# Turning q in 32x32 blocks on VectorE instead of by TensorE and DMA, in an attention + maxout kernel

## The chip, the cores and the metric

One core of a Trainium2 chip. The metric is the device time of one execution in microseconds (us), the median of several. Where I give a start or a duration from a profile, it is one profiled execution of that kernel. Engines: PE is TensorE, PEld its weight loads, DVE VectorE, ACT ScalarE, POOL GpSimd, SP SyncE.

## The reference

Eight batches of low-rank attention, followed by a maxout feed-forward layer over the same tokens. Cut to what matters:

```python
# q, k, v: [8 batches, 8 heads, 1024 tokens, 64] float32;  E, F: [64, 1024]
k_proj = einsum('ks,bhsd->bhkd', E, k)          # 1024 keys become 64
v_proj = einsum('ks,bhsd->bhkd', F, v)
scores = q @ k_proj^T / 8                       # contraction over d = 64
attn   = softmax(scores) @ v_proj
x      = attn with heads side by side           # [8192, 512]
h      = max(x @ w1, x @ w2, x @ w3)            # w: [512, 768]
out    = h @ w_out                              # w_out: [768, 512]
```

The contraction of the scores runs over d. The kernel's score matmuls read q and the keys with d on the partitions (in the trace of the kernel before, a moving operand of 64x512: 64 d by 512 tokens). So q, which is loaded with tokens on the partitions, is turned until d lies there. How q is turned is what changes here.

## The kernel before

It is a software pipeline: while the feed-forward matmuls of batch b run, the attention of batch b+1 is slipped between them in numbered *slots*. In the stage studied here one slot follows each group of four layer-1 matmuls (one PSUM bank, 4 x 216 ns = 0.86 us). Layer 1 rotates through four PSUM banks (0 to 3), which ACT and DVE empty; attention uses banks 4 to 7. Batch 0 has its own start-up code, which the change leaves alone.

Before the change q is turned in two ways. Batch 1, whose q is the last of its three inputs to be loaded, by 32 PE transposes through PSUM; batches 2 to 7 by DMA transposes, two per batch, issued by SP:

```python
def q_turn(b, hs):                                    # batches 2 to 7
    nc.sync.dma_start_transpose(
        out=qT[b % NB][:, hs].rearrange("p h s t -> p (h s) t"),
        in_=q_t[b % NB][:, hs].rearrange("p h si d -> p (h si d)"))

def q_pe1(hh):                                        # batch 1, two calls
    for h in range(4 * hh, 4 * hh + 4):
        for sp in range(SI // 2):
            o = (h % 2) * 512 + sp * P
            nc.tensor.transpose(out=psb[:, AB + (h % 4) // 2, o:o + P],
                                in_=q_t[1][:, h, 2 * sp:2 * sp + 2, :].rearrange("p s d -> p (s d)"), identity=ident)
    for j in range(2):                                # PSUM to SBUF, one on ACT, one on DVE
        (nc.vector.tensor_copy if j else nc.scalar.copy)(
            out=qT[1][:, ...], in_=psb[:, AB + j, :])
```

Keys and scores. The 64 projected keys leave PSUM twice, so that a copy lies on either half of the partitions after a DMA transpose; a score group is 8 matmuls in a 64x64 tiling (two waves of four tiles; in the trace the four of a wave start 3 to 4 ns apart, and the second wave 240 ns after the first):

```python
def kv():
    # ... 16 matmuls: keys to partitions 0-63, values to 64-127 of bank AB = 4
    nc.scalar.copy(out=kp2[i][:, :, 0, :], in_=kv_k)          # ACT, from PSUM
    nc.vector.tensor_copy(out=kp2[i][:, :, 1, :], in_=kv_k)   # DVE, from PSUM
    turn(i)                                                   # SP: DMA transpose kpT <- kp2
    nc.scalar.copy(out=vp2[i][KP:P], in_=kv_v[:, 1])
    nc.vector.tensor_copy(out=vp2[i][0:KP], in_=kv_v[:, 0])

def scores(u):
    for gg in range(2):
        g = 2 * u + gg
        for par in range(2):
            r = slice(par * D, (par + 1) * D)
            for col in range(2):
                h = HEAD[2 * g + col]
                nc.tensor.matmul(out=ps[col * KP:(col + 1) * KP, AB + 2 * gg + par, :],
                                 lhsT=kpT[i][r, h, :], rhs=qT[i][r, h, :, :], start=True, stop=True)
    # ... Exp on ACT, two instructions
```

Layer 1 and its evictions, and the schedule of batch 1's attention:

```python
# l1: four matmuls into one of four banks, then
if i == 0:   nc.scalar.copy(out=h1s[jt % 2], in_=ps[:, bank, :])                                        # ACT
elif i == 1: nc.vector.tensor_tensor(out=m12[jt % 2], in0=ps[:, bank, :], in1=h1s[jt % 2], op=ALU.max)  # DVE
else:        nc.vector.tensor_tensor(out=hT[c % 2][:, jt, :], in0=ps[:, bank, :], in1=m12[jt % 2], op=ALU.max)

# b == 0: (slot, work); g1[0] is kv of batch 1, g1[1] and g1[2] its two score groups
groups = [..., (20, g1[0]), (22, lambda: q_pe1(0)), (24, lambda: q_pe1(1)), (25, g1[1]), (28, g1[2]), ...]
```

The softmax here doesn't subtract the row's maximum and nothing guards it: scores larger than these inputs give would overflow.

Of the kernel before, what the change touches and what calls it, by code (L numbers as in the profile page):

```python
# [16 lines left out]
def kernel(ctx: ExitStack, tc: tile.TileContext, q, k, v, E, F, w1, w2, w3, w_out, out):  # L17
    nc = tc.nc
# [30 lines left out]
    q_t = [T([P, H, SI, D], BF16, f"q_t{i}") for i in range(NB)]  # L49
    qT = [T([P, H, SI // 2, P], BF16, f"qT{i}") for i in range(NB)]  # L50
    kp2 = [T([KP, H, 2, D], BF16, f"kp2_{i}") for i in range(NB)]
    kpT = [T([P, H, KP], BF16, f"kpT{i}") for i in range(NB)]
    vp2 = [T([P, NPAIR, 2, D // 2], BF16, f"vp2_{i}") for i in range(NB)]
    pT = T([P, NPAIR, 2, 512], BF16, "pT")
    xT = [T([P, NCT, 2, 512], BF16, f"xT{i}") for i in range(3)]
    lns = [T([P, 1024], FP32, f"lns{i}") for i in range(2)]
# [18 lines left out]

    out_v = out.rearrange("(b p sp par) m -> b par p sp m", p=P, sp=SI // 2, par=2)
    out_0 = out.rearrange("(b ch m t) n -> b ch m t n", ch=2, m=P, t=4)[0]
# [11 lines left out]
    def load_behind_turn(b, order="qkv"):  # L89

        nc.gpsimd.tensor_copy(out=seen, in_=kpT[(b - 1) % NB][:, 0, 0:1])
        for c in order:
            load(b, *{"q": (q, q_t), "k": (k, k_t), "v": (v, v_t)}[c])

    def q_turn(b, hs):
        nc.sync.dma_start_transpose(
            out=qT[b % NB][:, hs].rearrange("p h s t -> p (h s) t"),
            in_=q_t[b % NB][:, hs].rearrange("p h si d -> p (h si d)"),
        )
# [11 lines left out]
    def attention(b, turn):  # L111
        i = b % NB

        def kv():
            for si in range(SI):
                nc.tensor.matmul(out=ps[0:KP, AB, :], lhsT=eT[:, si, :], rhs=k_t[i][:, :, si, :],  # L116
                                 start=(si == 0), stop=(si == SI - 1))
                nc.tensor.matmul(out=ps[KP:P, AB, :], lhsT=fT[:, si, :], rhs=v_t[i][:, :, si, :],  # L118
                                 start=(si == 0), stop=(si == SI - 1))
            kv_k = ps[0:KP, AB, :].rearrange("p (h d) -> p h d", d=D)  # L120
            kv_v = ps[KP:P, AB, :].rearrange("p (g u dd f) -> p u g f dd", u=2, f=2, dd=HD)
            nc.scalar.copy(out=kp2[i][:, :, 0, :], in_=kv_k)  # L122
            nc.vector.tensor_copy(out=kp2[i][:, :, 1, :], in_=kv_k)  # L123
            turn(i)
            nc.scalar.copy(out=vp2[i][KP:P], in_=kv_v[:, 1])
            nc.vector.tensor_copy(out=vp2[i][0:KP], in_=kv_v[:, 0])

        def scores(u):
            for gg in range(2):
                g = 2 * u + gg  # L130
                for par in range(2):
                    r = slice(par * D, (par + 1) * D)
                    for col in range(2):
                        h = HEAD[2 * g + col]
                        nc.tensor.matmul(out=ps[col * KP:(col + 1) * KP, AB + 2 * gg + par, :],  # L135
                                         lhsT=kpT[i][r, h, :], rhs=qT[i][r, h, :, :], start=True, stop=True)
            for gg in range(2):
                nc.scalar.activation(out=pT[:, 2 * u + gg, :, :], in_=ps[:, AB + 2 * gg:AB + 2 * gg + 2, :],  # L138
                                     func=AF.Exp, scale=scale)

# [16 lines left out]
        def av(half):  # L157
            quads(lambda rows, g: vp2[i][rows, g, half, :])
            for u in range(2):
                nc.vector.tensor_tensor(out=xT[b % 3][:, 2 * u + half, :, :], in0=ps[:, AB + 2 * u:AB + 2 * u + 2, :],  # L160
                                        in1=rinv[u].rearrange("p (c n) -> p c n", c=2), op=ALU.mult)
# [4 lines left out]
    def turn_dma(i):  # L166
        nc.sync.dma_start_transpose(out=kpT[i], in_=kp2[i].rearrange("p h c d -> p (h c d)"))

# [7 lines left out]
    def l1(b, ch, c, jt, i):  # L176
        bank = fbank()
        for ct in range(NCT):
            nc.tensor.matmul(out=ps[:, bank, :], lhsT=w_sb[i][:, ct, jt * P:(jt + 1) * P],  # L179
                             rhs=xT[b % 3][:, ct, ch, :], start=(ct == 0), stop=(ct == NCT - 1))  # L180
        if i == 0:
# [50 lines left out]
    def k_proj0(g):  # L232
        for si in range(SI):
            for u in range(2):
                nc.tensor.matmul(out=ps[u * D:(u + 1) * D, 2, g * KP:(g + 1) * KP], lhsT=k_t[0][:, HEAD[2 * g + u], si, :],
                                 rhs=eT[:, si, :], start=(si == 0), stop=(si == SI - 1))
        nc.vector.tensor_copy(out=kpT[0][:, g, :], in_=ps[:, 2, g * KP:(g + 1) * KP])

# [7 lines left out]
    def scores0(ch, g, bank):  # L246
        for u in range(2):
            rows = slice(u * D, (u + 1) * D)
            nc.tensor.matmul(out=ps[u * KP:(u + 1) * KP, bank, :], lhsT=kpT[0][rows, g, :],  # L249
                             rhs=qT[0][rows, 4 * ch + g, :, :], start=True, stop=True)  # L250

# [20 lines left out]
    def q_up0():  # L272
# [5 lines left out]
        for j in range(2):  # L278
            (nc.vector.tensor_copy if j else nc.scalar.copy)(
                out=qT[0][:, 4 + 2 * j:6 + 2 * j].rearrange("p h s t -> p (h s t)"),  # L280
                in_=ps[:, 4 + 2 * j:6 + 2 * j, :].rearrange("p b n -> p (b n)"))
# [7 lines left out]
    def av_up0():  # L289
# [3 lines left out]
        norm0(1, 1, 4, (0, 1))  # L293


    def q_pe1(hh):
        for h in range(4 * hh, 4 * hh + 4):
            for sp in range(SI // 2):
                o = (h % 2) * 512 + sp * P
                nc.tensor.transpose(out=psb[:, AB + (h % 4) // 2, o:o + P],  # L300
                                    in_=q_t[1][:, h, 2 * sp:2 * sp + 2, :].rearrange("p s d -> p (s d)"), identity=ident)
        for j in range(2):
            (nc.vector.tensor_copy if j else nc.scalar.copy)(
                out=qT[1][:, 4 * hh + 2 * j:4 * hh + 2 * j + 2].rearrange("p h s t -> p (h s t)"), in_=psb[:, AB + j, :])

# [49 lines left out]
    def q_turn0(g):  # L355
        for n in range(4):
            nc.tensor.transpose(out=psb[:, 4 + g, n * P:(n + 1) * P],
                                in_=q_0[:, n, 2 * g:2 * g + 2, :].rearrange("p h d -> p (h d)"), identity=ident)
        nc.vector.tensor_copy(out=qT[0][:, g].rearrange("p s t -> p (s t)"), in_=psb[:, 4 + g, 0:512])

# [87 lines left out]
    for b in range(B):  # L448
        groups = attention(b + 1, turn_dma) if b + 1 < B else []
        if b == 0:  # L450
            g1 = [g for _, g in groups]
            groups = [(9, scores_up0), (12, lambda: sums0(1, 4)), (20, g1[0]), (22, lambda: q_pe1(0)), (24, lambda: q_pe1(1)), (25, g1[1]), (28, g1[2]),
                      (31, g1[3]), (32, g1[4]), (33, g1[5]), (34, g1[6]), (36, g1[7])]
# [3 lines left out]
        def tick():  # L457
# [5 lines left out]
            if b == 0:  # L463
                if slot == 22:
                    load_behind_turn(2, "kvq")
                if slot == 28:
                    q_turn(2, slice(0, H // 2))
                return
            if b == 1 and slot == 3:
                q_turn(2, slice(H // 2, H))  # L470
            if b + 2 < B:
                if slot == 9:
                    load_behind_turn(b + 2)
                if slot == 18:
                    q_turn(b + 2, slice(0, H // 2))
                if slot == 27:
                    q_turn(b + 2, slice(H // 2, H))

# [58 lines left out]
```

## Time and profile before

| | before |
|---|---|
| median time | 400.27 us (400.25 to 400.53, 3 runs) |
| span of the profiled run | 398.1 us |
| PE busy | 392.5 us, 99% of the span |
| steady period of one batch | 46.70 us |
| from batch 1's keys to batch 2's keys | 27.05 us |
| from batch 2's keys to batch 3's keys | 41.52 us |
| batch 1's keys to the last matmul | 346.81 us |

The last four rows are distances between starts of the same matmuls, which don't depend on how long the loads at the start took.

From the profile page of the kernel before, the busy time of each engine and three of the rows of tenths by slice of the span (9 is 90% or more):

```profile
PE 392.5 (99%) x2432; PEld 170.0 (43%) x2432; DVE 186.9 (47%) x269; ACT 166.0 (42%) x249; POOL 71.6 (18%) x110
...
PE   8999999999999999999999999999999999999996
...
DVE  3347355453834365443843266342654338433441
...
PEclk9999999999999999999999999999999999999999
```

PE has no idle slice at full clock, and DVE is half idle. The same page's row of DMA queue 1 (packets, MB, share of 16 engines), its chain of work by engine, and the DVE row of the second key copy (busy us, mean ns, then idle time before and its releaser):

```profile
q1 hardware_dynamic: 30032, 8.92, 15.3%
...
PE 95%; DMA 2%; DVE 1%; ACT 0%; POOL 0%; issue 0%; POOLq 0%; DVEq 0%
...
L123 DVE CAST kp<-ps 64x512 bf16<-64x512 f32 x7 | 4.8, 683 | 12.6 <-ACT kp L122 12.6
```

The chain that ended last is 95% PE, so a saving off PE is worth nothing unless it removes a PE wait. In the view of groups of instructions by form, the PE transposes and the score matmuls of the kernel before:

```profile
L135 PE MATMUL ps<-qT,kpT 64*64 64x512 bf16 x112 | 8.8, 388 | 0.0
...
L300 PE MATMUL ps<-ident,q_t 128*128 128x128 bf16 x32 | 2.1, 219 | 0.4 <-DVE vp L126 0.4
```

PE never waits before the scores (idle 0.0), and waits 0.4 us before the transposes. The timeline of PE in the stage of batch 1's attention (start, us, engine, line, operation, count, and idle time just before):

```profile
49.64 1.90 PE L179 MATMUL ps<-xT,w_sb 128*128 128x512 bf16 x8
51.95 1.05 PE L300 MATMUL ps<-ident,q_t 128*128 128x128 bf16 x16 [0.42 <-DVE vp L126]
52.84 1.89 PE L179 MATMUL ps<-xT,w_sb 128*128 128x512 bf16 x8
54.57 1.06 PE L300 MATMUL ps<-ident,q_t 128*128 128x128 bf16 x16
55.47 1.03 PE L179 MATMUL ps<-xT,w_sb 128*128 128x512 bf16 x4
56.42 0.63 PE L135 MATMUL ps<-qT,kpT 64*64 64x512 bf16 x8
```

The two transpose groups cost 0.89 us each (51.95 to 52.84), and the first one waits for the bank that the keys and values leave (the releaser is the value copy, L126). These 2.2 us are all that the change can take from PE.

### The profile page before, as it was taken

The page shows a single profiled execution, that of the slowest core. Times are in us where ns is not written, and L with a number is a line of the kernel's source. Part 1 is how long each engine was busy: PE and PEld are TensorE (multiplying, and loading weights), DVE is VectorE, ACT ScalarE, POOL GpSimd, SP SyncE. Part 2 cuts the span into 40 slices and gives each one's busy share as a digit, 9 for nine tenths or more (in the row PEclk, how much of TensorE's full clock was granted, in tenths as well). Part 3 has the DMA queues.
Part 4 walks back from the last instruction along what each step waited for, and adds up shares of the span by engine and source line. Part 5 has one row for each costly group of instructions (what it writes and reads, how often), then busy time and mean ns, then how long its engine had stood idle before and what let it go on. Part 6 is the DMA issues. An engine that isn't in the chain of part 4 may idle for free.

```text
span 398.1 us, 6013 instructions
## 1 busy us (share of the span) xinstructions
PE 392.5 (99%) x2432; PEld 170.0 (43%) x2432; DVE 186.9 (47%) x269; ACT 166.0 (42%) x249; POOL 71.6 (18%) x110
## 2 busy tenths in 40 slices
PE   8999999999999999999999999999999999999996
PEld 4444443444444444444444444444444444444443
DVE  3347355453834365443843266342654338433441
ACT  3414457347225642347223662245522472222222
POOL 6452140150003300060000600033010000000000
PEclk9999999999999999999999999999999999999999
DMA  8999979999912998169920999129992111102022
GB/s 225 206 209 206 207 172 195 240 162 185 191 54 72 187 197 174 34 116 186 239 95 13 173 197 213 54 67 180 220 131 63 55 53 54 53 7 100 1 107 105
DMA packets 62667, 53.73 MB, mean 135 GB/s; under 512 B 30512, under 2 KB 57648, under 8 KB 62640
## 3 DMA queue, kind: packets, MB, share of 16 engines
q0 software_dynamic: 31776, 43.52, 53.8%
q1 hardware_dynamic: 30032, 8.92, 15.3%
q10 hardware_dynamic: 832, 0.92, 0.7%
q8 instruction: 19, 0.31, 0.3%
q14 instruction: 8, 0.07, 0.0%
HBM read 57.15 MB, written 16.78 MB: 186 GB/s over the span
## 4 chain that ended last, share of the span: by engine, by line
PE 95%; DMA 2%; DVE 1%; ACT 0%; POOL 0%; issue 0%; POOLq 0%; DVEq 0%
PE ps L179 59%; PE ps L203 19%; PE ps L116 3%; PE ps L145 3%; PE ps L407 2%; DMA k_t<-in_k_dram 2%; PE ps L135 2%; PE ps L398 1%; PE ps L216 1%; PE ps L308 1%; PE ps L229 1%; DVE xT L160 1%; PE ps L249 1%; PE ps L300 0%; PE ps L242 0%; PE ps L196 0%
## 5 line engine op out<-in xcount | busy, mean ns | idle before, releaser
L179 PE MATMUL ps<-xT,w_sb 128*128 128x512 bf16 x1080 | 246.3, 379 | 0.0
L179 PEld LDWEIGHTS <-w_sb 128*128 128x128 bf16 x1080 | 103.2, 98 | 132.1 <-issue 12.0
L184 DVE TENSOR_TENSOR m<-ps,h1s 128x512 f32<-128x512 f32 x90 | 62.2, 691 | 143.8 <-PE ps L179 124.5
L203 PE MATMUL ps<-wo_sb,hT 128*128 128x512 bf16 x354 | 85.5, 379 | 0.0
L182 ACT COPY h1s<-ps 128x512 f32<-128x512 f32 x90 | 52.8, 587 | 66.8 <-PE ps L179 66.5
L205 ACT COPY o_acc<-ps 128x512 f32<-128x512 f32 x59 | 34.6, 587 | 97.8 <-PE ps L203 97.8
L210 POOL DMA_DIRECT2D out_dram<-o_acc x28 | 20.1, 720 | 271.1 <-ACT o_acc L205 271.1
L186 DVE TENSOR_TENSOR hT<-ps,m 128x512 bf16<-128x512 f32 x90 | 62.3, 692 | 13.7 <-PE ps L179 5.2
L203 PEld LDWEIGHTS <-hT 128*128 128x128 bf16 x354 | 33.6, 98 | 44.1 <-issue 5.4
L160 DVE TENSOR_TENSOR xT<-ps,rinv 128x1024 bf16<-128x1024 f32 x28 | 32.9, 1218 | 7.8 <-PE ps L145 7.8
L138 ACT ACTIVATE pT<-ps 128x1024 bf16<-128x1024 f32 x28 | 27.1, 1022 | 13.3 <-PE ps L135 13.3
L87 POOL DMA_DIRECT2D v_t<-in_v_dram x21 | 15.3, 750 | 4.0 <-DMA q_t<-in_q_dram 2.0
L152 ACT ACTIVATE lns<-ps 128x1024 f32<-128x1024 f32 x14 | 13.6, 1022 | 1.9 <-PE ps L145 1.9
L155 ACT ACTIVATE rinv<-lns 128x1024 f32<-128x1024 f32 x14 | 14.2, 1061 | 0.0
L116 PE MATMUL ps<-k_t,eT 128*64 128x512 bf16 x56 | 13.4, 382 | 0.0
L118 PE MATMUL ps<-v_t,fT 128*64 128x512 bf16 x56 | 13.4, 382 | 0.0
L87 POOL DMA_DIRECT2D q_t<-in_q_dram x14 | 10.6, 767 | 3.2 <-DMA wo_sb<-in_moe_w_out_dram 1.1
L87 POOL DMA_DIRECT2D k_t<-in_k_dram x14 | 10.5, 762 | 2.2 <-ACT o_acc L445 1.2
L407 PE MATMUL ps<-xT,w_sb 128*128 128x512 bf16 x48 | 10.9, 379 | 0.0
L123 DVE CAST kp<-ps 64x512 bf16<-64x512 f32 x7 | 4.8, 683 | 12.6 <-ACT kp L122 12.6
L308 PE MATMUL ps<-warm 128*128 128x512 bf16 x26 | 9.4, 469 | 1.2 <-DVE ones L340 1.2
L122 ACT CAST kp<-ps 64x512 bf16<-64x512 f32 x7 | 4.1, 580 | 14.1 <-PE ps L118 14.1
(85 smaller groups left out, 155.5 us busy)
## 6 DMA issues: line engine op xcount, KB each, us to landing
out_dram<-o_acc POOLq DMA_DIRECT2D x30, 512.0 KB, 3.3
q_t<-in_q_dram POOLq DMA_DIRECT2D x15, 512.0 KB, 8.5
k_t<-in_k_dram POOLq DMA_DIRECT2D x14, 512.0 KB, 13.4
v_t<-in_v_dram POOLq DMA_DIRECT2D x18, 256.0 KB, 17.6
v_t<-in_v_dram POOLq DMA_DIRECT2D x7, 512.0 KB, 16.8
w_sb<-in_moe_w_dram POOLq DMA_DIRECT2D x4, 384.0 KB, 10.1
k_t<-in_k_dram POOLq DMA_DIRECT2D x4, 256.0 KB, 8.4
w_sb<-in_moe_w_dram POOLq DMA_DIRECT2D x4, 192.0 KB, 9.6
```

What stands on the lines that cost most here:

```text
L87: nc.gpsimd.dma_start(out=dst[b % NB][:, slots], in_=sv[:, heads])
L116: nc.tensor.matmul(out=ps[0:KP, AB, :], lhsT=eT[:, si, :], rhs=k_t[i][:, :, si, :], start=(si == 0), stop=(si == SI - 1))
L138: nc.scalar.activation(out=pT[:, 2 * u + gg, :, :], in_=ps[:, AB + 2 * gg:AB + 2 * gg + 2, :], func=AF.Exp, scale=scale)
L160: nc.vector.tensor_tensor(out=xT[b % 3][:, 2 * u + half, :, :], in0=ps[:, AB + 2 * u:AB + 2 * u + 2, :], in1=rinv[u].rearrange("p (c n) -> ...
L179: nc.tensor.matmul(out=ps[:, bank, :], lhsT=w_sb[i][:, ct, jt * P:(jt + 1) * P], rhs=xT[b % 3][:, ct, ch, :], start=(ct == 0), stop=(ct == ...
L182: nc.scalar.copy(out=h1s[jt % 2], in_=ps[:, bank, :])
L184: nc.vector.tensor_tensor(out=m12[jt % 2], in0=ps[:, bank, :], in1=h1s[jt % 2], op=ALU.max)
L186: nc.vector.tensor_tensor(out=hT[c % 2][:, jt, :], in0=ps[:, bank, :], in1=m12[jt % 2], op=ALU.max)
L203: nc.tensor.matmul(out=ps[:, bank, :], lhsT=hT[c % 2][:, jt, tt * P:(tt + 1) * P], rhs=wo_sb[:, jt, :], start=(jt == 0), stop=(jt == NJT - 1))
L205: nc.scalar.copy(out=o[:, tt, :], in_=ps[:, bank, :])
L210: nc.gpsimd.dma_start(out=dst[:, tt - 1:tt + 1, :], in_=o[:, tt - 1:tt + 1, :])
L407: nc.tensor.matmul(out=ps[:, bank, :], lhsT=w_sb[i][:, ct, jt * P:(jt + 1) * P], rhs=xT[0][:, ct, 0, :], start=(ct == 0), stop=(ct == NCT ...
```

## The change

Intent: take the turning of q off TensorE and off the DMA queues, and give it to DVE, which is half idle. The kernel calls DVE's transpose and is written for a result that is turned in blocks of 32x32 words. It passes a pair of neighbouring bf16 values of d as one 4-byte word, so the 64 d of a head and token are 32 words: one block row. As the code reads it after the flip, each group of 32 partitions holds the 32 d pairs of its own 32 tokens, with even and odd d interleaved along the free dimension. The scores must follow this layout: four row groups of 32 partitions and two heads as columns make eight 32x64 tiles; each group is two accumulating passes (even d, odd d), and the moving operand of a pass has stride 2. The keys must lie on all four row groups, with even and odd d apart, so four copies are needed: the keys leave PSUM once (ACT), and DVE makes the other three copies within SBUF.

Core of the diff (cut: renaming of layouts, the order of the output rows, the PSUM layout that Exp reads, one buffer of xT fewer; the two Exp take 1.02 us each before and after):

```diff
-    def q_turn(b, hs):
-        nc.sync.dma_start_transpose(...)
+    def q_flip(b, g):
+        hs = slice(2 * g, 2 * g + 2)                       # two heads
+        nc.vector.transpose(
+            out=qT[b % NB][:, hs].bitcast(FP32).rearrange("p h n -> p (h n)"),
+            in_=q_t[b % NB][:, hs].rearrange("p h si d -> p (h si d)").bitcast(FP32),
+        )
 ...
-            nc.scalar.copy(out=kp2[i][:, :, 0, :], in_=kv_k)
-            nc.vector.tensor_copy(out=kp2[i][:, :, 1, :], in_=kv_k)
+            nc.scalar.copy(out=kp2[i][:, :, :, 0, :], in_=kv_k)
+            nc.vector.tensor_copy(out=kp_[:, :, 1:], in_=kp_[:, :, 0:1].to_broadcast([KP, 2 * H, 3, HD]))
 ...  scores, per g:
-                for par in range(2):
-                    for col in range(2):
-                        nc.tensor.matmul(... 64x64 tile, 512 columns, start=True, stop=True)
+                for f in range(2):
+                    for r in range(4):
+                        rows = slice(r * HD, (r + 1) * HD)
+                        for col in range(2):
+                            h = HEAD[2 * g + col]
+                            nc.tensor.matmul(out=ps[col * KP:(col + 1) * KP, AB + r, gg * 256:(gg + 1) * 256],
+                                             lhsT=kpT[i][rows, h, f, :],
+                                             rhs=qT[i][rows, h].rearrange("p (n f) -> p n f", f=2)[:, :, f],
+                                             start=(f == 0), stop=(f == 1), tile_position=(r * HD, col * KP))
 ...
-    def q_pe1(hh): ...
 ...  schedule of batch 1's attention:
-            groups = [..., (20, g1[0]), (22, lambda: q_pe1(0)), (24, lambda: q_pe1(1)), (25, g1[1]), (28, g1[2]),
+            groups = [..., (20, g1[0]),
+                      (22, lambda: q_flip(1, 0)), (23, lambda: q_flip(1, 1)), (25, g1[1]), (26, lambda: q_flip(1, 2)),
+                      (27, lambda: q_flip(1, 3)), (28, g1[2]),
 ...  batches 2 to 7: the DMA transposes go; flips in slots 4 to 7 (batch 2) and 32, 34, 36, 38 (the others)
```

More of the change, by code (lines that the diff above doesn't have):

```diff
@@ L49 @@
     q_t = [T([P, H, SI, D], BF16, f"q_t{i}") for i in range(NB)]
-    qT = [T([P, H, SI // 2, P], BF16, f"qT{i}") for i in range(NB)]
-    kp2 = [T([KP, H, 2, D], BF16, f"kp2_{i}") for i in range(NB)]
-    kpT = [T([P, H, KP], BF16, f"kpT{i}") for i in range(NB)]
+    qT = [T([P, H, SI * D], BF16, f"qT{i}") for i in range(NB)]
+    kp2 = [T([KP, H, 2, 4, D // 2], BF16, f"kp2_{i}") for i in range(NB)]
+    kpT = [T([P, H, 2, KP], BF16, f"kpT{i}") for i in range(NB)]
     vp2 = [T([P, NPAIR, 2, D // 2], BF16, f"vp2_{i}") for i in range(NB)]
     pT = T([P, NPAIR, 2, 512], BF16, "pT")
-    xT = [T([P, NCT, 2, 512], BF16, f"xT{i}") for i in range(3)]
+    xT = [T([P, NCT, 2, 512], BF16, f"xT{i}") for i in range(2)]
     lns = [T([P, 1024], FP32, f"lns{i}") for i in range(2)]
@@ L72 @@
     h1c = [o_acc[1][:, j, :] for j in range(4)] + [h1s[0], h1s[1]]
-    out_v = out.rearrange("(b p sp par) m -> b par p sp m", p=P, sp=SI // 2, par=2)
+    out_v = out.rearrange("(b p ch t) m -> b ch p t m", p=P, ch=2, t=4)
     out_0 = out.rearrange("(b ch m t) n -> b ch m t n", ch=2, m=P, t=4)[0]
@@ L89, in load_behind_turn @@
     def load_behind_turn(b, order="qkv"):
-        nc.gpsimd.tensor_copy(out=seen, in_=kpT[(b - 1) % NB][:, 0, 0:1])
+        nc.gpsimd.tensor_copy(out=seen, in_=kpT[(b - 1) % NB][:, 0, 0, 0:1])
         for c in order:
             load(b, *{"q": (q, q_t), "k": (k, k_t), "v": (v, v_t)}[c])
-    def q_turn(b, hs):
-        nc.sync.dma_start_transpose(
-            out=qT[b % NB][:, hs].rearrange("p h s t -> p (h s) t"),
-            in_=q_t[b % NB][:, hs].rearrange("p h si d -> p (h si d)"),
+    def q_flip(b, g):
[3 more added lines that the diff above has]
+            in_=q_t[b % NB][:, hs].rearrange("p h si d -> p (h si d)").bitcast(FP32),
         )
@@ L119, in kv @@
                                  start=(si == 0), stop=(si == SI - 1))
-            kv_k = ps[0:KP, AB, :].rearrange("p (h d) -> p h d", d=D)
+            kv_k = ps[0:KP, AB, :].rearrange("p (h dd f) -> p h f dd", dd=HD, f=2)
             kv_v = ps[KP:P, AB, :].rearrange("p (g u dd f) -> p u g f dd", u=2, f=2, dd=HD)
-            nc.scalar.copy(out=kp2[i][:, :, 0, :], in_=kv_k)
-            nc.vector.tensor_copy(out=kp2[i][:, :, 1, :], in_=kv_k)
+            kp_ = kp2[i].rearrange("k h f r dd -> k (h f) r dd")
+            nc.scalar.copy(out=kp2[i][:, :, :, 0, :], in_=kv_k)
+            nc.vector.tensor_copy(out=kp_[:, :, 1:], in_=kp_[:, :, 0:1].to_broadcast([KP, 2 * H, 3, HD]))
             turn(i)
@@ L130, in scores @@
                 g = 2 * u + gg
-                for par in range(2):
-                    r = slice(par * D, (par + 1) * D)
-                    for col in range(2):
-                        h = HEAD[2 * g + col]
-                        nc.tensor.matmul(out=ps[col * KP:(col + 1) * KP, AB + 2 * gg + par, :],
-                                         lhsT=kpT[i][r, h, :], rhs=qT[i][r, h, :, :], start=True, stop=True)
+                for f in range(2):
[7 more added lines that the diff above has]
+                                             start=(f == 0), stop=(f == 1), tile_position=(r * HD, col * KP))
             for gg in range(2):
-                nc.scalar.activation(out=pT[:, 2 * u + gg, :, :], in_=ps[:, AB + 2 * gg:AB + 2 * gg + 2, :],
-                                     func=AF.Exp, scale=scale)
+                nc.scalar.activation(
+                    out=pT[:, 2 * u + gg].rearrange("p ch (t r n) -> p r (ch t) n", t=4, r=4),
+                    in_=ps[:, AB:AB + 4, gg * 256:(gg + 1) * 256].rearrange("p r (si n) -> p r si n", si=SI),
+                    func=AF.Exp, scale=scale)
         def quads(lhs):
@@ L159, in av @@
             for u in range(2):
-                nc.vector.tensor_tensor(out=xT[b % 3][:, 2 * u + half, :, :], in0=ps[:, AB + 2 * u:AB + 2 * u + 2, :],
+                nc.vector.tensor_tensor(out=xT[b % 2][:, 2 * u + half, :, :], in0=ps[:, AB + 2 * u:AB + 2 * u + 2, :],
                                         in1=rinv[u].rearrange("p (c n) -> p c n", c=2), op=ALU.mult)
@@ L166, in turn_dma @@
     def turn_dma(i):
-        nc.sync.dma_start_transpose(out=kpT[i], in_=kp2[i].rearrange("p h c d -> p (h c d)"))
+        nc.sync.dma_start_transpose(out=kpT[i].rearrange("p h f k -> p (h f) k"), in_=kp2[i].rearrange("k h f r dd -> k (h f r dd)"))
     state = {"f": 0, "n": 0}
@@ L179, in l1 @@
             nc.tensor.matmul(out=ps[:, bank, :], lhsT=w_sb[i][:, ct, jt * P:(jt + 1) * P],
-                             rhs=xT[b % 3][:, ct, ch, :], start=(ct == 0), stop=(ct == NCT - 1))
+                             rhs=xT[b % 2][:, ct, ch, :], start=(ct == 0), stop=(ct == NCT - 1))
         if i == 0:
@@ L236, in k_proj0 @@
                                  rhs=eT[:, si, :], start=(si == 0), stop=(si == SI - 1))
-        nc.vector.tensor_copy(out=kpT[0][:, g, :], in_=ps[:, 2, g * KP:(g + 1) * KP])
+        nc.vector.tensor_copy(out=kpT[0][:, g, 0, :], in_=ps[:, 2, g * KP:(g + 1) * KP])
     def v_proj0(g, bank):
@@ L248, in scores0 @@
             rows = slice(u * D, (u + 1) * D)
-            nc.tensor.matmul(out=ps[u * KP:(u + 1) * KP, bank, :], lhsT=kpT[0][rows, g, :],
-                             rhs=qT[0][rows, 4 * ch + g, :, :], start=True, stop=True)
+            nc.tensor.matmul(out=ps[u * KP:(u + 1) * KP, bank, :], lhsT=kpT[0][rows, g, 0, :],
+                             rhs=qT[0][rows, 4 * ch + g, :], start=True, stop=True)
     def exp0(ch, g, bank):
@@ L279, in q_up0 @@
             (nc.vector.tensor_copy if j else nc.scalar.copy)(
-                out=qT[0][:, 4 + 2 * j:6 + 2 * j].rearrange("p h s t -> p (h s t)"),
+                out=qT[0][:, 4 + 2 * j:6 + 2 * j].rearrange("p h n -> p (h n)"),
                 in_=ps[:, 4 + 2 * j:6 + 2 * j, :].rearrange("p b n -> p (b n)"))
@@ L293, in av_up0 @@
         norm0(1, 1, 4, (0, 1))
-    def q_pe1(hh):
-        for h in range(4 * hh, 4 * hh + 4):
-            for sp in range(SI // 2):
-                o = (h % 2) * 512 + sp * P
-                nc.tensor.transpose(out=psb[:, AB + (h % 4) // 2, o:o + P],
-                                    in_=q_t[1][:, h, 2 * sp:2 * sp + 2, :].rearrange("p s d -> p (s d)"), identity=ident)
-        for j in range(2):
-            (nc.vector.tensor_copy if j else nc.scalar.copy)(
-                out=qT[1][:, 4 * hh + 2 * j:4 * hh + 2 * j + 2].rearrange("p h s t -> p (h s t)"), in_=psb[:, AB + j, :])
     def warmup(n, bank):
@@ L358, in q_turn0 @@
                                 in_=q_0[:, n, 2 * g:2 * g + 2, :].rearrange("p h d -> p (h d)"), identity=ident)
-        nc.vector.tensor_copy(out=qT[0][:, g].rearrange("p s t -> p (s t)"), in_=psb[:, 4 + g, 0:512])
+        nc.vector.tensor_copy(out=qT[0][:, g], in_=psb[:, 4 + g, 0:512])
     def q_cast0(g):
@@ L451 @@
             g1 = [g for _, g in groups]
-            groups = [(9, scores_up0), (12, lambda: sums0(1, 4)), (20, g1[0]), (22, lambda: q_pe1(0)), (24, lambda: q_pe1(1)), (25, g1[1]), (28, g1[2]),
+            groups = [(9, scores_up0), (12, lambda: sums0(1, 4)), (20, g1[0]),
+                      (22, lambda: q_flip(1, 0)), (23, lambda: q_flip(1, 1)), (25, g1[1]), (26, lambda: q_flip(1, 2)),
+                      (27, lambda: q_flip(1, 3)), (28, g1[2]),
                       (31, g1[3]), (32, g1[4]), (33, g1[5]), (34, g1[6]), (36, g1[7])]
@@ L465, in tick @@
                     load_behind_turn(2, "kvq")
-                if slot == 28:
-                    q_turn(2, slice(0, H // 2))
                 return
-            if b == 1 and slot == 3:
-                q_turn(2, slice(H // 2, H))
+            if b == 1 and slot in (4, 5, 6, 7):
+                q_flip(2, slot - 4)
             if b + 2 < B:
@@ L473, in tick @@
                     load_behind_turn(b + 2)
-                if slot == 18:
-                    q_turn(b + 2, slice(0, H // 2))
-                if slot == 27:
-                    q_turn(b + 2, slice(H // 2, H))
+                if slot in (32, 34, 36, 38):
+                    q_flip(b + 2, slot // 2 - 16)
         for ch in range(2):
```

## The prediction

> **What bounds the kernel now.** TensorE. On the profile page PE is busy 99% of the span (392.5 of 398.1 us), and the chain of work that ended last is 95% PE. In the timeline of the steady stage (from about 76 us) the full-array matmuls start 216 ns apart without a gap, whatever the DMA share is, and one batch takes 46.7 us. PE does not wait for the DMA transposes of q. So only PE time and new PE waits can move the total.
>
> **What goes.**
> - The 32 PE transposes of q for batch 1 (two groups of 16, 56 ns apart: 2 x 0.89 us) and the 0.42 us that PE waits before the first. Worth at most 2.2 us, all on the chain.
> - Twelve DMA transposes of q (most of queue 1's 15% of DMA time). Nothing on the chain waits for them: worth 0.
> - The second PSUM read of the keys (DVE, 683 ns x 7), off the chain.
>
> **What comes.**
> - Scores: 32 matmuls of 256 columns a group in place of 8 of 512. Eight tiles at once instead of four; per group four waves of about 110 ns instead of two of 215. The trace shows tiles of one wave starting 3 ns apart, and each change of tiling costs about 0.09 us on entry and on exit, as before. So about equal: +0.03 us a group, +0.4 us in all. The stride-2 moving operand is the doubt.
> - Four block transposes per batch on DVE, 1024 fp32 elements per partition each. [...] with the fixed ~0.15 us that the trace shows for DVE operations, I estimate 1.25 us each, 5 us a batch, 35 us in all (DVE from 47% to about 55%). The trace has no such operation.
> - The key copy in SBUF (bf16, 1536 elements): estimate 0.55 us, like the 0.68 us it replaces. The key transpose by DMA doubles: estimate 1 to 1.3 us later (3.7 us now in batch 1's stage).
>
> **How much lies on the critical path.** DVE also empties the layer-1 banks; four banks rotate, so PE stalls when DVE runs about 2 us late. I walked through DVE's order with the measured durations:
> - Steady stage (transposes behind the second normalisation, slots 32 to 38): backlog at most about 2 us, every bank free just in time (0.3 to 0.6 us to spare). No stall.
> - Batch 1's attention (50 to 60 us): four transposes (5 us) replace 1.4 us of DVE copies, just ahead of the scores. First scores wait for the transposes and the later keys: about 1.8 us; second scores about 1.3 us. This eats the 2.2 us; net +0.8 us.
> - Batch 2's transposes (slots 4 to 7, 79 to 86 us): four back to back among bank evictions; PE stalls about 1.1 us on banks.
>
> **Sum.** 400.3 - 2.2 + 3.0 + 1.1 + 0.4 = 402.6 us. Range 399.5 to 408. Chances: faster 0.02, same 0.84, slower 0.14.
>
> **What would show it.** Transposes near 1.25 us in the groups; score groups still about 0.55 us first start to next full-array matmul; PE waits on DVE's transposes or the keys near 54 to 60 us and on evictions near 82 to 86 us; steady batches still 46.7 us; DMA queue 1 down to some 7,000 packets.
>
> **What would make it wrong.** [...] Or the queues hide the stalls: 399 us.

The sum came to 402.6 us, and its +3.0 and +1.1 rest on the 1.25 us. That figure is left as an estimate because the trace of the kernel before gives nearly the same: DVE's operations from PSUM with 256, 512 and 1024 fp32 elements per partition take 426, 691 and 1218 ns there (L126, L184, L160), which is 0.16 us and 1.03 ns an element. They are not transposes; that a transpose would take as long was an assumption. The "about 2 us" by which DVE may run late is an estimate of the walk too; in the run with every flip done twice, four flips held DVE for 2.78 us and PE stalled 1.2 us.

## The result, and the profile after

| | before | after |
|---|---|---|
| median | 400.40 us (400.25 to 400.63, 4 runs) | 400.59 us (400.54 to 400.63, 4 runs) |
| ratio after / before | | 1.0004, 95% interval 0.9987 to 1.0022 |
| span of the profiled run | 398.1 us | 398.7 us |
| batch 1's keys to batch 2's keys | 27.05 us | 26.91 us |
| batch 2's keys to batch 3's keys | 41.52 us | 41.59 us |
| steady period | 46.70 us | 46.77 us |
| batch 1's keys to the last matmul | 346.81 us | 347.07 us |

A ratio is the mean time of one kernel's runs over that of the other's of the same rounds, so it is not quite the ratio of the medians quoted. Executions over 1.5% slower than the fastest of the same kernel are left out of the means. The time lies in the predicted range, but 2 us below the predicted value, and the two kernels cannot be told apart by the clock.

From the profile page of the kernel after, the busy times, queue 1, the chain by engine, and the new DVE instruction:

```profile
PE 391.4 (98%) x2736; PEld 171.4 (43%) x2736; DVE 200.1 (50%) x295; ACT 163.6 (41%) x247; POOL 66.6 (17%) x110
...
q1 hardware_dynamic: 8656, 3.54, 4.4%
...
PE 90%; DMA 6%; DVE 2%; ACT 1%; issue 1%; POOL 0%; POOLq 0%; DVEq 0%
...
L99 DVE STREAM_TRANSPOSE qT<-q_t 128x512 f32<-128x512 f32 x28 | 19.3, 695 | 0.0
```

The chain's DMA share rose from 2% to 6%, but 3 points of that are a weight load in the start-up, which the change does not touch; 1 point is the keys' DMA. In the view of groups by form of the kernel after, the scores and the key copy:

```profile
L140 PE MATMUL ps<-qT,kpT 32*64 32x256 bf16 x448 | 9.5, 277 | 1.9 <-DMA kpT<-kp 1.1 <-DVE qT L99 0.8
...
L127 DVE COPY kp<-kp 64x1536 bf16<-64x1536 bf16 x7 | 3.9, 552 | 12.6 <-ACT kp L126 12.6
```

PE now waits 1.9 us before the scores where it waited 0.0, for two things: 1.1 us for the keys' DMA transpose, 0.8 us for a flip. Both waits fall once. The timeline of PE in batch 1's attention shows where:

```profile
49.61 4.49 PE L188 MATMUL ps<-xT,w_sb 128*128 128x512 bf16 x20
55.15 0.66 PE L140 MATMUL ps<-qT,kpT 32*64 32x256 bf16 x32 [1.05 <-DMA kpT<-kp]
55.75 2.76 PE L188 MATMUL ps<-xT,w_sb 128*128 128x512 bf16 x12
58.44 0.43 PE L140 MATMUL ps<-qT,kpT 32*64 32x256 bf16 x16
59.70 0.43 PE L140 MATMUL ps<-qT,kpT 32*64 32x256 bf16 x16 [0.82 <-DVE qT L99]
```

Twenty layer-1 matmuls now run without a break where two transpose groups stood between them, and then PE stands still. The chain that ended last in the same stage (start, us, what) says what it stood still for:

```profile
49.75 0.59 ACT kp L126
50.33 0.02 issue
50.36 0.04 DVE kp L127
50.39 0.54 issue
50.94 4.17 DMA kpT<-kp
55.11 0.04 issue
55.15 0.71 PE ps L140 x31
55.86 0.02 issue
55.88 1.94 ACT pT L145 x2
57.82 0.49 ACT h1s L191
58.31 0.02 issue
58.34 0.69 DVE m L193
59.03 0.63 DVE qT L99
```

Read from the top: the keys leave PSUM, are copied, and their DMA transpose is issued at 50.94 and lands at 55.11, 4.17 us later. Only then can the first scores run. Their two Exp instructions hold ACT for 1.94 us, so ACT's eviction of the next layer-1 bank (h1s) comes late, so DVE's eviction that needs it (m) comes late, and the last flip of batch 1 stands behind that eviction in DVE's program order. The second score group waits for that flip. DVE was idle for 2.25 us in front of that eviction: DVE did not lack time, it was blocked by order.

**The account.** Take the same full-array matmul in both traces and subtract its distance from batch 1's keys, before from after:

| step | after minus before, us |
|---|---|
| 32 PE transposes and the wait in front of them gone | -2.37 |
| first scores of batch 1 wait for the keys | +1.16 |
| second scores of batch 1 wait for the last flip | +1.06 |
| 12 score groups of batches 2 to 7 at +0.033 | +0.40 |
| sum of the rows | +0.25 |
| measured, batch 1's keys to the last matmul | +0.26 |

(The two waits are start-to-start differences, so they are a little larger than the idle times of the profile and include the growth of batch 1's own two score groups. The steady period grew by 0.07 us, which is the growth of its two score groups, so the other parts of the change, one buffer of xT fewer among them, cost PE nothing there.) The removed work was on the critical path and is truly gone; two new waits in the same 10 us gave 2.2 us back.

### The profile page after: what moved, and what is told of

It is laid out like the page before. It is cut to its first block, busy times and chain, and to the rows that moved or that the text cites. A ratio compares the mean times of both kernels' runs of the same rounds, so it can differ in the third digit from the quotient of the medians.

```text
span 398.7 us, 6631 instructions
## 1 busy us (share of the span) xinstructions
PE 391.4 (98%) x2736; PEld 171.4 (43%) x2736; DVE 200.1 (50%) x295; ACT 163.6 (41%) x247; POOL 66.6 (17%) x110
## 4 chain that ended last, share of the span: by engine, by line
PE 90%; DMA 6%; DVE 2%; ACT 1%; issue 1%; POOL 0%; POOLq 0%; DVEq 0%
PE ps L188 57%; PE ps L212 19%; PE ps L119 3%; PE ps L154 3%; DMA w_sb<-in_moe_w_dram 3%; PE ps L405 2%; PE ps L140 2%; DMA k_t<-in_k_dram 2%; PE ps L225 1%; PE ps L396 1%; DMA kpT<-kp 1%; DVE xT L169 1%; ACT pT L145 0%; PE ps L238 0%; PE ps L205 0%
## 5 line engine op out<-in xcount | busy, mean ns | idle before, releaser
L193 DVE TENSOR_TENSOR m<-ps,h1s 128x512 f32<-128x512 f32 x90 | 62.1, 690 | 135.5 <-PE ps L188 117.0
L219 POOL DMA_DIRECT2D out_dram<-o_acc x28 | 15.3, 546 | 275.0 <-ACT o_acc L214 266.0
L169 DVE TENSOR_TENSOR xT<-ps,rinv 128x1024 bf16<-128x1024 f32 x28 | 32.9, 1218 | 7.5 <-PE ps L154 7.5
L99 DVE STREAM_TRANSPOSE qT<-q_t 128x512 f32<-128x512 f32 x28 | 19.3, 695 | 0.0
L140 PE MATMUL ps<-qT,kpT 32*64 32x256 bf16 x448 | 9.5, 277 | 1.9 <-DMA kpT<-kp 1.1
```

Source lines behind the costliest of these rows:

```text
L99: nc.vector.transpose(out=qT[b % NB][:, hs].bitcast(FP32).rearrange("p h n -> p (h n)"), in_=q_t[b % NB][:, hs].rearrange("p h si d -> p ( ...
L169: nc.vector.tensor_tensor(out=xT[b % 2][:, 2 * u + half, :, :], in0=ps[:, AB + 2 * u:AB + 2 * u + 2, :], in1=rinv[u].rearrange("p (c n) -> ...
```

## The experiments

Twelve kernels ran, in three jobs on three chips, each job with its own 9 runs of the kernel before (medians 400.13, 400.21 and 400.15 us). One caution: all twelve passed the comparison with the reference, including four which are wrong (they compute scores from zeros, from stale q or from a wrong order of q). So the comparison does not see an error in the scores, and it is no proof either that the new layout of the scores is right; that rests on reading the code. These four are experiments on time only.

Theory A: the change takes 2.2 us of PE work from batch 1's stage, and the late keys and a blocked flip give it back; the DMA transposes are worth nothing. Rivals: the DMA transposes' departure gains something that slower scores eat; or the flips load DVE as I had predicted, and something unseen compensates.

### Removing each old way of turning q alone

The kernel before without the PE transposes (batch 1's q zeros):

```diff
+    nc.gpsimd.memset(qT[1], 0.0)
-            groups = [..., (20, g1[0]), (22, lambda: q_pe1(0)), (24, lambda: q_pe1(1)), (25, g1[1]), ...
+            groups = [..., (20, g1[0]), (25, g1[1]), ...
```

> The kernel before without its 32 PE transposes of q of batch 1 (wrong result on purpose; that q buffer is filled with zeros by GpSimd). Theory 1 (the removal is real PE time, given back later by the change's own new waits): PE reaches the first scores of batch 1 about 2.3 us sooner, then waits about 0.6 us there for the keys' DMA transpose, which lands near 54.7 us; total 1.5 to 1.9 us less than before, about 398.6 us. Rival (batch 1's stage is bound by the keys or by DVE, so that the PE transposes only fill time that is idle anyway): within 0.4 us of before.

Measured: 400.5 us, the median of four runs (399.93 to 400.90), ratio 1.0008 (0.9994 to 1.0021); the fifth run was slow (406.39 us). No gain, against the theory. The trace shows that the gain was made and mostly lost again: batch 1's stretch is 25.21 us, 1.84 less than before, but batch 2's stretch is 42.74 us, 1.22 more. From batch 1's keys to the last matmul 0.63 us stay (346.18 us), which the times of whole runs don't show; they spread over 1 us. The timeline of PE and then of SP's queue in this run:

```profile
75.63 6.64 PE L179 MATMUL ps<-xT,w_sb 128*128 128x512 bf16 x30
83.41 0.63 PE L135 MATMUL ps<-qT,kpT 64*64 64x512 bf16 x8 [1.15 <-DMA kpT<-kp]
```

```profile
72.15 4.24 SPq L96 DMA_TRANSPOSE qT<-q_t  x1
76.64 2.31 SPq L167 DMA_TRANSPOSE kpT<-kp  x1
79.06 19.69 SPq L96 DMA_TRANSPOSE qT<-q_t  x2
```

With PE ahead, the keys' DMA transpose of batch 2 is issued at 76.64 us, while the big DMA transpose of q is still under way in the same queue, and lands 6.7 us later instead of the median of 2.6. So the DMA transposes of q were not free in every case: they cost nothing only as long as PE was slower.

The kernel before without the DMA transposes (batches 2 to 7 use stale q; `q_turn` returns at once):

```diff
     def q_turn(b, hs):
+        return
         nc.sync.dma_start_transpose(
```

> The kernel before without the 12 DMA transposes of q (wrong result on purpose, stale q). Theory 1 (worth nothing: no step of the chain waits for them): total within 0.2 us of before, PE start to start 216 ns and a batch every 46.7 us as before. Rival (DMA traffic or SBUF traffic of the transposes slows the matmuls or the loads): 0.5 us or more less.

Measured: 400.30 us, ratio 1.0002 (0.9988 to 1.0016), and the stretches are 27.05, 41.52 and 46.70 us, to the last digit those of before. Alone, this removal takes nothing off, as the prediction said. Both removals together:

```diff
     def q_turn(b, hs):
+        return
 ...
+    nc.gpsimd.memset(qT[1], 0.0)
-            groups = [..., (20, g1[0]), (22, lambda: q_pe1(0)), (24, lambda: q_pe1(1)), (25, g1[1]), ...
+            groups = [..., (20, g1[0]), (25, g1[1]), ...
```

> The kernel before without the PE transposes of batch 1 and without the DMA transposes of q (wrong result on purpose, zeros and stale q). Without the PE transposes alone the stretch from batch 1's keys to batch 2's keys fell from 27.05 to 25.21 us, but the next stretch grew from 41.52 to 42.74, where PE waited for batch 2's keys, whose DMA transpose stood in the queue behind that of q. Theory (two things have to go together: the PE transposes are worth 1.8 us only if the DMA transposes of q leave the queue too): 25.2 and 41.5 us, so 1.8 us less than before from the first keys to the last matmul, about 398.4 us. Rival (something else holds batch 2's scores): the second stretch stays above 42.3 us.

Measured: 398.70 us, ratio 0.9962 (0.9949 to 0.9976). From batch 1's keys to the last matmul it takes 345.12 us, 1.69 less than before; batch 2's stretch is back at 41.52. PE's timeline:

```profile
54.95 0.63 PE L136 MATMUL ps<-qT,kpT 64*64 64x512 bf16 x8 [0.61 <-DMA kpT<-kp]
```

What follows: 1.7 us is what both removals are worth together. Alone, that of the DMA transposes is worth 0, and that of the PE transposes 0.63 us in the trace and nothing that the times of whole runs show. It is not the full 2.37 us because even here PE waits 0.61 us for the keys in batch 1. The change (347.07) stands 1.95 us above this, which is what its additions cost.

### Is it the length of the flips?

The kernel after, with every flip done twice:

```diff
-        nc.vector.transpose(...)
+        for _ in range(2):
+            nc.vector.transpose(...)
```

> The changed kernel with each VectorE transpose done twice (right result), which makes a slot cost the 1.25 us that the prediction took for one. Theory 1 (the only wrong term of the prediction was the size of one transpose, 0.695 us measured; the walk through the four rotating banks was right): about 402.4 us, 1.5 to 2.5 us over the changed kernel: batch 1's second scores wait about 0.5 to 0.7 us longer, batch 2's stage (79 to 86 us) stalls on banks by about 1.1 us, steady batches keep their period. Rival A (the banks hide it too): within 0.7 us of the changed kernel. Rival B (backlog in every batch): 4 us or more over it.

Measured: 402.67 us (402.44 to 402.86), ratio 1.0063 (1.0050 to 1.0076). Two flips (1.42 us: 0.725 from the first start to the second, then 0.70) are a little more than the 1.25 us that I had estimated for one, and the time is close to the predicted 402.6. The timeline of PE in batch 2's stage, where I had predicted bank stalls of 1.1 us, and then of DVE:

```profile
83.69 1.02 PE L189 MATMUL ps<-xT,w_sb 128*128 128x512 bf16 x4 [0.19 <-DVE hT L196]
84.64 0.66 PE L141 MATMUL ps<-qT,kpT 32*64 32x256 bf16 x32
85.24 1.04 PE L189 MATMUL ps<-xT,w_sb 128*128 128x512 bf16 x3
86.97 3.61 PE L189 MATMUL ps<-xT,w_sb 128*128 128x512 bf16 x16 [0.69 <-DVE m L194]
```

```profile
83.56 2.78 DVE L100 STREAM_TRANSPOSE qT<-q_t 128x512 f32<-128x512 f32 x4
86.26 0.65 DVE L194 TENSOR_TENSOR m<-ps,h1s 128x512 f32<-128x512 f32 x1
```

Four flips in a row hold DVE for 2.78 us, the bank evictions behind them come late, and PE stalls: start to start 0.35 + 0.86 = 1.2 us, against the predicted 1.1. In batch 1 the wait for the flip grows from 0.82 to 1.57 us, and the wait for the keys hardly changes (1.05 to 1.10). The steady period stays at 46.77 us. So the reasoning about DVE's order was right in this stage and its input was wrong: with a flip of 0.695 us there is no stall in batch 2.

### What the new form of the scores costs

The kernel after, with the moving operand contiguous (wrong order of q, same shapes and counts), one look:

```diff
-                                             rhs=qT[i][rows, h].rearrange("p (n f) -> p n f", f=2)[:, :, f],
+                                             rhs=qT[i][rows, h, f * 256:(f + 1) * 256],
```

> The changed kernel with the moving operand of the scores read as 256 elements in a row instead of every second one (wrong result on purpose). In the changed kernel a score group takes 0.594 us from its first matmul to the next full-array one, against 0.556 us before, and its waves of eight matmuls start 115 ns apart. Theory 1 (the extra 0.04 us is four waves instead of two, not the stride): 0.594 us and 115 ns again. Rival (the stride costs): waves 110 ns or less apart and 0.57 us or less.

Measured: 400.37 us in a single run, whose state is unknown, so only the trace counts. A score group, from its first matmul to the next full-array one, takes 575 ns here, 592 in the change and 558 before (medians of the groups without a wait); the later waves of eight tiles start 109 ns apart, against 115 with stride 2. Both theories were half right: of the 34 ns by which a group grew, half are the stride and half the four waves in place of two. Over 14 groups that is about 0.24 us each.

The entry to a score group is 309 ns from the last full-array matmul, where two of those follow each other at 216: 93 ns more at the change of tiling. It was the same in all three kernels, and so for the two tilings entered here, 64x64 and 32x64.

### The wait for the last flip

The kernel after, with the last flip of batch 1 one slot earlier, ahead of the blocked eviction:

```diff
-                      (27, lambda: q_flip(1, 3)), (28, g1[2]),
+                      (26, lambda: q_flip(1, 3)), (28, g1[2]),
```

> The changed kernel with the last VectorE transpose of batch 1 put one slot earlier, ahead of a bank eviction that waits for PE. Theory (the 0.8 us that the second scores of batch 1 wait is program order on VectorE, not VectorE's load): the wait goes, 0.8 us less than the changed kernel from the first keys to the last matmul. Rival (VectorE is full there): the wait stays or turns up at an eviction, 0.2 us or less.

Measured: 399.77 us (399.63 to 399.80), ratio to before 0.9987 (0.9974 to 1.0001), by the ratios (1.0004 and 0.9987, since the change ran in another job) 0.7 us below the change. The second wait is gone from the trace, where the second score group now runs in one piece:

```profile
55.23 0.66 PE L140 MATMUL ps<-qT,kpT 32*64 32x256 bf16 x32 [0.48 <-DMA kpT<-kp]
58.52 0.66 PE L140 MATMUL ps<-qT,kpT 32*64 32x256 bf16 x32
```

In the profiled run batch 1's keys happened to come 0.65 us later, which shortened the first wait to 0.48 us, so its 345.47 us from the keys to the end shows more than this edit.

### The wait for the keys

The kernel after, with the keys one slot (0.86 us) earlier:

```diff
-            groups = [(9, scores_up0), (12, lambda: sums0(1, 4)), (20, g1[0]),
+            groups = [(9, scores_up0), (12, lambda: sums0(1, 4)), (19, g1[0]),
```

> The changed kernel with the key and value projections of batch 1 one slot (0.86 us) earlier. Theory (the first scores wait 1.1 us for the chain keys, copy, DMA transpose): their wait shrinks to about 0.3 us, the second wait stays near 0.8 us, total 0.85 us less than the changed kernel, about 399.7 us. Rival (they wait for the VectorE transposes): no gain.

Measured: 400.67 us, ratio 1.0011 (0.9997 to 1.0025): nothing, against my expectation. SP's queue and the timeline of PE of this run:

```profile
50.08 1.31 SPq L176 DMA_TRANSPOSE kpT<-kp  x1
```

```profile
55.18 0.66 PE L140 MATMUL ps<-qT,kpT 32*64 32x256 bf16 x32 [1.07 <-DMA kpT<-kp]
```

The transpose was issued at 50.08 instead of 50.94, and the scores still began at 55.18. So something at a fixed time held the keys. The record of single DMA packets shows what did: 256 packets of 4096 bytes, half of batch 0's output (1 MB, issued by GpSimd at 44.00 and 45.29 us), run from 49.8 to 53.6 us in both kernels, and the first of the keys' 1056 packets starts at 52.4 us in the change and at 52.3 in this run, 1.42 and 2.20 us after the issue. In the six later batches of the change it starts 1.17 us after the issue. So SP's small transpose seemed to wait behind GpSimd's store, although another engine had issued that; the run with the store held back, below, tests it.

With both edits together:

```diff
-                      (27, lambda: q_flip(1, 3)), (28, g1[2]),
+                      (26, lambda: q_flip(1, 3)), (28, g1[2]),
-            groups = [..., (20, g1[0]),
+            groups = [..., (19, g1[0]),
```

> Both moves in one kernel (right result). Theory (the two waits are what the change gave back): 1.6 to 1.9 us less than the changed kernel, about 398.7 us, faster than both kernels by 0.4%. Rival (a later step of batch 1, the sums or the second normalisation, binds then): less than 1 us.

Measured: 399.71 us (399.47 to 399.89), ratio 0.9985 (0.9971 to 0.9998), like the flip's edit alone, and half of the gain that I had expected. The first wait is still there:

```profile
55.25 0.66 PE L140 MATMUL ps<-qT,kpT 32*64 32x256 bf16 x32 [1.05 <-DMA kpT<-kp]
```

This run and the one before differ by the last flip's slot alone, and both have the keys at the same slot: from batch 1's keys to the last matmul it is 346.93 against 347.95 us, so the flip's slot is worth 1.02 us in the trace, and 0.96 us in the medians of the same job (400.67 to 399.71).

The test of the store: last flip at 26, keys left at 20, and the first output store held back until the keys have landed.

```diff
+    held = []
     def load_behind_turn(b, order="qkv"):
         nc.gpsimd.tensor_copy(out=seen, in_=kpT[(b - 1) % NB][:, 0, 0, 0:1])   # waits for the keys
+        while held:
+            tt = held.pop(0)
+            nc.gpsimd.dma_start(out=out_0[0][:, tt - 1:tt + 1, :], in_=o_acc[0][:, tt - 1:tt + 1, :])
 ...
-                nc.gpsimd.dma_start(out=out_0[0][:, tt - 1:tt + 1, :], in_=o_acc[0][:, tt - 1:tt + 1, :])
+                held.append(tt)
```

> The changed kernel with the last VectorE transpose early and with the first 1 MB of output stored behind batch 1's key transpose instead of ahead of it (right result). Moving the keys 0.86 us earlier did not move their landing (55.2 us both times), and their 256-byte packets start only as the 4096-byte packets of that store drain (50.5 to 53 us). Theory (the keys' DMA transpose waits for DMA engines that are full with that store and the rest of the loads): the keys land near 54.4 us, the first scores wait 0.5 us or less instead of 1.1, total 0.6 us less than with the early transpose alone, about 399.2 us. Rival (the landing is set by the doubled size of the transpose or by the loads alone): no change.

Measured: 398.86 us (398.85 to 399.78), ratio 0.9975 (0.9959 to 0.9990). PE's timeline:

```profile
54.34 0.66 PE L145 MATMUL ps<-qT,kpT 32*64 32x256 bf16 x32 [0.43 <-DMA kpT<-kp]
```

The store was the cause of the late start: without it the keys' packets start 1.24 us after their issue (50.75 to 51.99) and land after 3.55 us, as in the other batches of the change (median 3.5) and not after 4.17. The wait falls from 1.05 to 0.43 us. What is left is the length of the keys' own path. Now the earlier slot should pay, since the keys are no longer held by something else. All three edits together, that is, on top of the last diff:

```diff
-            groups = [..., (20, g1[0]),
+            groups = [..., (19, g1[0]),
```

> As the last run, with the keys one slot earlier too (right result). Theory: now the earlier keys count: they land near 53.6 us, before PE needs them, and nothing waits in batch 1's scores; the stretch from the first keys to the last matmul is about 345.8 us (346.9 with the two moves alone), total about 398.6 us, 0.4% under the kernel before. Rival (full queue by the loads): no better than the two moves alone, 399.7 us.

Measured: 398.45 us (398.29 to 398.54), ratio 0.9956 (0.9944 to 0.9969). PE's timeline:

```profile
53.96 0.66 PE L145 MATMUL ps<-qT,kpT 32*64 32x256 bf16 x32
...
57.25 0.66 PE L145 MATMUL ps<-qT,kpT 32*64 32x256 bf16 x32
```

No wait is left in batch 1's scores. The interval lies wholly below 1: this version beats both kernels, by 1.7 us against the kernel before of the same job (400.15). The slot that gained nothing behind the store took the last 0.43 us of waiting away here (medians 398.86 to 398.45).

### Controls on the kernel before

If earlier keys pay by themselves, then they should pay in the old form too, and part of the above would not belong to the change.

```diff
-            groups = [(9, scores_up0), (12, lambda: sums0(1, 4)), (20, g1[0]), (22, lambda: q_pe1(0)), ...
+            groups = [(9, scores_up0), (12, lambda: sums0(1, 4)), (19, g1[0]), (22, lambda: q_pe1(0)), ...
```

> The kernel before with batch 1's keys one slot earlier (right result), to see what the old form gains from the same care. Theory (its PE transposes wait 0.4 to 0.6 us for VectorE to leave the bank of the keys; a slot earlier that wait goes, but batch 2's keys stand behind the DMA transposes of q as in the run without PE transposes): 0 to 0.5 us less than before. Rival (it gains as much as the changed kernel with all its moves, so the change as such is worth nothing): 1.2 us or more.

Measured: 399.50 us (399.44 to 400.03), ratio 0.9986 (0.9972 to 1.0000). In the trace PE no longer waits before the transposes, and batch 1's stretch is 0.57 us shorter than before once the slot (0.86 us) is taken off. That is all that the keys could hold up there. Batch 2's keys did not come to stand behind the DMA transposes of q, as I had feared: that stretch stays at 41.52 us.

Finally the key copy alone, from SBUF instead of PSUM, in the kernel before:

```diff
-            nc.vector.tensor_copy(out=kp2[i][:, :, 1, :], in_=kv_k)
+            nc.vector.tensor_copy(out=kp2[i][:, :, 1, :], in_=kp2[i][:, :, 0, :])
```

> The kernel before with the second copy of the keys read from SBUF instead of PSUM (right result): this part of the change alone. Theory (off the chain): within 0.2 us of before, the copy near 0.3 us instead of 0.68. Rival (the eviction of keys was on the way of the next work): 0.4 us or more less.

Measured: 399.48 us (399.14 to 400.06), ratio 0.9984 (0.9970 to 0.9998), against an expectation of nothing. The copy takes 285 ns instead of 683, so DVE's copy of the values, the last reader of the bank, comes sooner, and the transposes don't wait: batch 1's stretch is 26.47 us, 0.58 less. The PSUM read that the prediction called off the chain was in front of PE in one batch of seven. Its 0.4 us was nevertheless in the prediction's 2.2 us, as PE's wait, so it changes no term of the sum. These two controls also say how to read the 1.7 us above: against the old form with its own small repair (399.48 and 399.50 us in the same job) the best version is ahead by 1.0 us. Whether the old form gains from holding the store back was not tried.

## Why the prediction was wrong and where it was right

| term of the sum | predicted, us | measured, us |
|---|---|---|
| PE transposes and the wait before them | -2.2 | -2.37 |
| batch 1's scores wait | +3.0 | +2.2 (profile: 1.05 + 0.82) |
| batch 2's banks stall | +1.1 | 0 |
| score groups | +0.4 | +0.40 (12 groups; batch 1's two are in the row of its waits) |
| sum | +2.3 | +0.25 (+0.26 from the first keys to the last matmul in the trace; +0.2 in the medians) |

**The step that failed** is "four block transposes per batch on DVE, 1024 fp32 elements per partition each ... I estimate 1.25 us each". A flip takes two heads of 8 x 64 bf16, which is 1024 bf16 values but only 512 fp32 words. I counted values where I should have counted words. The measured flip is 0.695 us (one that follows another directly starts 0.62 us after it), and all 28 take 19.3 us where I had 35. The time per word was not the error: the 0.16 us and 1.03 ns an element of the three DVE operations named beside the prediction give an estimate of 0.69 us for 512 words, and the flip takes as long as another DVE operation on 512 elements, the eviction L193 at 690 ns.

**What followed from it.** Batch 2's stall of 1.1 us did not come. Batch 1's waits were nearer to 1.1 + 1.1 than to 1.8 + 1.3, and for other reasons than I gave: the first was for the keys alone (the flips of the first scores ended at 54.1 us, the keys at 55.1), and the second was no shortage of DVE time but the order of its program. So in batch 1 the mechanism failed too, and not only the size. Of the 2.0 us by which the sum was too high, 1.1 is batch 2, 0.8 is batch 1's waits, and the rest is the removed work, which was worth a little more than I said.

**Shown by experiment.** Doubling the flips to what I had assumed brings back the batch 2 stall (1.2 us) and the predicted time (402.67). That the total fits so well is partly luck: batch 1's waits are 1.10 and 1.57 us there, where I had 1.8 and 1.3. That the late keys and the blocked flip are the two costs is shown by removing each: the flip one slot earlier takes off 0.7 us (1.0 us between the two kernels of one job that differ by it alone), and the store out of the keys' way together with the earlier slot takes off 1.2 more (ratios 0.9987 and 0.9956).

**Where it was right.** The bottleneck; the 2.2 us on PE; the DMA transposes of q worth nothing by themselves; the score groups (+0.033 us each against 0.03, though half of it is the stride that was only doubted); the copy in SBUF (0.552 us against 0.55, an estimate for which the prediction shows no working); no stall in steady batches; the keys landing later (median 2.6 to 3.5 us, 0.9 later against 1 to 1.3). The range held, but it is wide (8.5 us). That the change came out even is a coincidence of sizes: 2.37 us left PE, and two waits, in part of other origins, and the score groups happened to add up to 2.6.

**What it missed.** First, that the two removals depend on each other: without the DMA transposes' departure, most of the saving on PE would have been lost at batch 2 (1.22 of 1.84 us). The change as a whole has both, so this did not alter the sum. Second, that a store in front of the keys made them land late in batch 1: 0.6 of the 1.05 us of that wait went with the store, the rest with the earlier slot.

**Open.** The tail after the last matmul. It is 3.55 to 3.56 us in the four profiled kernels that keep the DMA transposes of q, and 3.79 to 3.83 us in the ten without them, the change among these. So some 0.25 us go with the removal of these transposes, outside the stretches of the tables. The last store has landed 2.5 us after the last matmul in all fourteen, so the difference lies behind it; why is not shown. With it the traces put the change 0.53 us behind, the medians 0.2; the start-up varies by up to 1 us, and the interval of the ratio (0.9987 to 1.0022) can't tell these apart.

## What to carry to other kernels

When work leaves the bottleneck engine, look at once for what has to be ready earlier because of it, and at what stands in front of that: here 2.4 us left PE, and a store, two activations and one eviction in the wrong order gave most of it back. A DMA that lands late need not be slow or issued late; look at which other packets run on the DMA engines between its issue and its first packet, and move those (here the first packet came 1.42 and 2.20 us after the issue behind the store, and 1.24 without it). And count the elements of an instruction after every bitcast: here 512 words and not 1024 values, 0.695 us and not 1.25.
